# Linear attention into a gated feed-forward, one core: new loading of batch 0, one load queue in the order of need, and a reordered first output stage

## The chip, the cores and the metric

The kernel runs on one NeuronCore of one Trainium2 chip. A time is the duration of one execution on the device in microseconds (us). Five engines run side by side, each through its own list of instructions in order: PE (TensorE, matrix products), DVE (VectorE), ACT (ScalarE), POOL (GpSimd) and SP (SyncE, which here only issues transfers). Sixteen DMA engines move data between the chip's main memory and the on-chip memory. A transfer is issued by an engine and lands some us later; transfers that change the type on the way (fp32 in memory, bf16 on chip) are issued by POOL in this kernel, plain ones by SP.

Times in the texts below are positions on the trace of one profiled execution, counted from its first instruction.

## What is computed

Linear attention with the feature map phi(x) = elu(x) + 1 over 8 batches, 8 heads, 576 rows and head size 64, and then a feed-forward layer of width 2048 with a gate whose slope beta is a vector.

```python
def phi(x):
    return np.where(x > 0, x, np.exp(x) - 1.0) + 1.0
q_p, k_p = (phi(q), phi(k))
kv = np.einsum('bhsd,bhse->bhde', k_p, v)
z = np.sum(k_p, axis=2)
num = np.einsum('bhsd,bhde->bhse', q_p, kv)
den = np.einsum('bhsd,bhd->bhs', q_p, z)[..., None] + 1e-06
x = (num / den).transpose(0, 2, 1, 3).reshape(B * S, H * D)   # 4608 x 512
h = x @ w_in                                                   # 512 x 2048
g = h * (1.0 / (1.0 + np.exp(-beta * h)))
out = g @ w_out                                                # 2048 x 512
```

All inputs are fp32. The products run in bf16.

## The kernel before

Each batch has 576 rows: four tiles of 128 rows, and a fifth of 64 rows. The fifth tiles of the eight batches are gathered in `xT_tail` and run as a ninth batch. The stages of batch b are called here: phi (of k and q), kv (the product of phi(k) and v), numer (phi(q) times kv, divided), x_trans (x transposed), H (x times w_in, 16 tiles of `h_ps`, each put through Silu by ACT) and Y (g times w_out, four output tiles of 16 products each). From batch 2 on, the attention of the next batch is threaded into H of the current one, and its phi into Y. Batches 0 and 1 have an order written by hand.

The loads at the start, by SP and by POOL:

```python
k0f = stage[:, 0 : 4 * J * D]...               # fp32, in the buffer of w_out quarters 2 and 3
def load(eng, dst, src, b, h0=0, n=4): ...     # one transfer; h0, n: pairs of heads

for h0 in (0, 2):
    load(nc.sync, k0f, k, 0, h0, 2)
nc.sync.dma_start(out=beta_row, in_=moe_beta...)
nc.vector.memset(warm, 0.5)
...
make_identity(nc, identity)                    # on POOL
for h0 in (0, 2):
    load(nc.gpsimd, xq[0], q, 0, h0, 2)        # cast to bf16
for h0 in (0, 2):
    load(nc.gpsimd, vb[0], v, 0, h0, 2)
w_in_dma = [nc.gpsimd.dma_start(out=w_in_sb[i], ...) for i in range(4)]
load_w_out(0, w_in_dma[1])                     # SP, fp32, held until w_in quarter 1 is there
load_w_out(1)
hold(load(nc.gpsimd, xk[1], k, 1), w_in_dma[3])
q1_dma = load(nc.gpsimd, xq[1], q, 1)
load(nc.gpsimd, vb[1], v, 1)
```

The start of batch 0. `idle(n)` gives PE n products that nobody reads, to keep it from standing still:

```python
phi_step("k", 0, phi_part); phi_step("k", 1, phi_part)      # ACT: exp
idle(14)
phi_step("k", 0, phi_relu); phi_step("k", 0, phi_min)       # DVE
phi_step("q", 0, phi_part); ...                             # ACT
phi_step("k", 1, phi_relu)
w_out2_dma = load_w_out(2, q1_dma)                          # SP, held until q of batch 1 is there
load_w_out(3)
phi_step("k", 1, phi_min)
zt = [num0_tile() for _ in range(2)]
z_products(0, 0, zt)                                        # PE: sums of phi(k)
nc.tensor.matmul(bps, beta_row, ident16, is_transpose=True) # PE: beta to columns
idle(4)
z_products(0, 1, zt)
nc.vector.tensor_copy(beta_s, bps)                          # DVE, then three more small ones
...
phi_step("q", 0, phi_relu)
z_evac(zt)
phi_step("q", 0, phi_min)
phi_step("q", 1, phi_relu)
phi_step("q", 1, phi_min, 0, 4); phi_step("q", 1, phi_min, 4, J)
idle(10)
q_trans0(0); q_trans0(1)                                    # PE transposes, ACT copies
kv_direct(0, 0, kvp0)                                       # PE: phi(k) times v
for hh in range(2): kv_evac(0, hh, (0,), kvp0)              # DVE
q_trans0(2)
...                                                         # kv_direct, kv_evac of pair 1
dens(0, (0, 1), dps); recips(0, 2, P, dps)
q_trans0(3)
numer0(0, 0); numer0(0, 1)
...
x_trans(0, 0, nc.scalar)
...                                                         # then H of batch 0
```

Two PSUM pools matter later. `num0ps` has two banks and serves batches 0 and 1; `numps` takes their place from batch 2 on and holds one tile:

```python
def num0_tile():
    return num0ps.tile([P, 512], F32, tag="num0", name="nps0")   # bufs=2
def recips(t0, t1, n, dps):          # den and 1/den of row tiles t0 to t1, read from dps
    ...
def numer0(b, t):
    nps = num0_tile()
    ...                              # four products on PE
    norm(b, t, n, nps..., rden0[:n, t])   # DVE: nps times 1/den -> xs
def x_trans(b, t, eng): ...          # PE transposes xs; eng copies to xT
```

The stretch of Y of batch 0 and the attention of batch 1:

```python
w_out_scale(0, 0); w_out_scale(1, 0)          # DVE: w_out by 1/beta, to bf16
yps = [mm_tile("y_ps") for _ in range(4)]     # the four banks that h_ps uses too
phi_all(1, "k"); phi_all(1, "q")
for i in range(2):
    for t in range(4):
        y_mm(0, t, i, yps[t])                 # quarter i of the sum of output tile t
...                                           # z_products, z_evac of batch 1; loads of batch 2
for ts in ((0, 1), (2, 3)): q_trans(1, ts, num0_tile()..., (nc.scalar, nc.scalar))
for pr in range(2): kv_direct(1, pr, kv1)
w_out_scale(2, 0)
...                                           # kv_evac
dps1 = num0_tile()
q_trans(1, (4,), dps1..., (nc.scalar,))
y_mm(0, 0, 2, yps[0])
dens(1, range(NT), dps1)
recips(0, 4, P, dps1); recips(4, 5, G, dps1)
y_mm(0, 1, 2, yps[1])
numer0(1, 0); numer0(1, 1)
w_out_scale(3, 2)
...                                           # y_mm, x_trans, numer0 in turn
numer0(1, 4)
...
phi_part(2, "q", pr, ...); phi_relu; phi_min(2, "q", 0); phi_part(2, "k", 0, ...)
...
```

In H of batch 1, run after its tile 0: `q_trans_dma(2)` and `x_trans(1, 4, nc.vector)`; `numer(2, t)` runs after tiles 7, 9, 11, 13 and 15.

Of the kernel before, what the change touches and what calls it, by code (L numbers as in the profile page):

```python
# [16 lines left out]
def kernel(  # L17
# [55 lines left out]
        for a in vf  # L73
    ]

    k0f = stage[:, 0 : 4 * J * D].rearrange("p (h j d) -> p h j d", h=4, j=J)

    def load(eng, dst, src, b, h0=0, n=4):

        rows = src[b].rearrange("h (g j) d -> (h g) (j d)", j=J)  # L80
        return eng.dma_start(  # L81
            out=dst[:, h0 : h0 + n].rearrange("p h j d -> p h (j d)"),
            in_=rows.rearrange("(i p) e -> p i e", p=P)[:, h0 : h0 + n],
        )
# [3 lines left out]


    beta_row = consts.tile([FC, P], F32)  # L90
    for h0 in (0, 2):
        load(nc.sync, k0f, k, 0, h0, 2)
    nc.sync.dma_start(out=beta_row, in_=moe_beta.rearrange("(c p) -> c p", p=P))
    nc.vector.memset(warm, 0.5)  # L94
    tiny = consts.tile([P, 2], BF16)
# [2 lines left out]
    make_identity(nc, identity)  # L98
    ident16 = consts.tile([FC, FC], F32)
    make_identity(nc, ident16)  # L100
    for h0 in (0, 2):
        load(nc.gpsimd, xq[0], q, 0, h0, 2)
    for h0 in (0, 2):
        load(nc.gpsimd, vb[0], v, 0, h0, 2)

    w_in_v = moe_w_in.rearrange("(c p) f -> p c f", p=P)
    w_out_v = moe_w_out.rearrange("(c p) m -> p c m", p=P)
    w_in_dma = [
        nc.gpsimd.dma_start(out=w_in_sb[i], in_=w_in_v[:, :, i * 512 : (i + 1) * 512])  # L109
        for i in range(4)  # L110
    ]

    def load_w_out(i, after=None):
        d = nc.sync.dma_start(out=w_out_f[i], in_=w_out_v[:, i * 4 : (i + 1) * 4, :])
        if after is not None:
            hold(d, after)
        return d

    load_w_out(0, w_in_dma[1])
    load_w_out(1)  # L120
    hold(load(nc.gpsimd, xk[1], k, 1), w_in_dma[3])
    q1_dma = load(nc.gpsimd, xq[1], q, 1)
    load(nc.gpsimd, vb[1], v, 1)

    kvmask = consts.tile([P, 2, 2, EA], BF16)
    nc.vector.memset(kvmask, 0.0)
    nc.vector.memset(kvmask[:D, :, 0, :], 1.0)
    nc.vector.memset(kvmask[D:P, :, 1, :], 1.0)
    ones = consts.tile([P, 2], BF16)
    nc.vector.memset(ones, 1.0)  # L130
    for i in range(2):
        nc.vector.memset(vaug[i][:, :, :, :, D : D + 2], 1.0)

    warm_ps = mmps.tile([P, 512], F32, tag="mm", name="warm_ps")

# [29 lines left out]
        )  # L165

    def xin(b, a, pr):
        if b == 0 and a == "k":
            return k0f[:, 2 * pr : 2 * pr + 2]
        return (xk if a == "k" else xq)[b % NX][:, 2 * pr : 2 * pr + 2]  # L170

    def v_copy(eng, b, pr):
# [186 lines left out]
    def rows(b, j):  # L359
        return out[b * S : (b + 1) * S, :].rearrange("(g j) m -> j g m", j=J)[j]  # L360

    def y_out(b, t, yp, c0=0, c1=512, queues=(nc.sync, nc.sync)):
        y_sb = work.tile([P, DM], F32, tag="y_sb", name="y_sb", bufs=3)
        nc.vector.tensor_copy(y_sb[:, c0:c1], yp[:, c0:c1])  # L364
        for i in range(2):
            dst = rows(b, 2 * t + i) if b < B else rows(2 * t + i, J - 1)
            queues[i].dma_start(out=dst[:, c0:c1], in_=y_sb[i * G : (i + 1) * G, c0:c1])
# [74 lines left out]
    def phi_step(a, pr, f, *r):  # L442
        f(0, a, pr, *((xin(0, a, pr),) if f is not phi_min else ()), *r)
# [11 lines left out]
    phi_step("q", 1, phi_part, 0, 4)  # L455
    phi_step("q", 1, phi_part, 4, J)
    phi_step("k", 1, phi_relu)
    w_out2_dma = load_w_out(2, q1_dma)
    load_w_out(3)
    phi_step("k", 1, phi_min)  # L460
    zt = [num0_tile() for _ in range(2)]
    z_products(0, 0, zt)
# [9 lines left out]
    z_evac(zt)  # L472
    phi_step("q", 0, phi_min)
    phi_step("q", 1, phi_relu)
    phi_step("q", 1, phi_min, 0, 4)
    phi_step("q", 1, phi_min, 4, J)
    idle(10)
# [1 line left out]
    def q_trans0(t):  # L479
        q_trans(0, (t,), misc_bf()[:, 0 : 512 if t < NT - 1 else 256], (nc.scalar,))  # L480

    q_trans0(0)
    q_trans0(1)
    kv_direct(0, 0, kvp0)
    for hh in range(2):
        kv_evac(0, hh, (0,), kvp0)
    q_trans0(2)
    kvp1 = [num0_tile() for _ in range(2)]
    kv_direct(0, 1, kvp1)
    for hh in range(2):  # L490
        kv_evac(0, hh, (1,), kvp1)
    dens(0, (0, 1), dps)
    recips(0, 2, P, dps)
    q_trans0(3)
    numer0(0, 0)
    numer0(0, 1)
# [30 lines left out]
    def w_out_scale(i, n_act):  # L527
        for c in range(4):
# [3 lines left out]
            else:  # L532
# [2 lines left out]
                    None, ALU.mult,  # L535
                )

    nc.vector.reciprocal(rbeta, beta_c)
    w_out_scale(0, 0)
    w_out_scale(1, 0)  # L540
    yps = [mm_tile("y_ps") for _ in range(4)]
    phi_all(1, "k")
    phi_all(1, "q")
# [2 lines left out]
            y_mm(0, t, i, yps[t])  # L546
    kv1 = [miscps.tile([P, 512], F32, tag="misc", name="kv1") for _ in range(2)]
    kv_tile(1)
    for pr in range(2):
        z_products(1, pr, kv1)  # L550
    z_evac(kv1)
    hold(load(nc.gpsimd, xq[2], q, 2), w_out2_dma)
    load(nc.gpsimd, xk[2], k, 2)
    load(nc.gpsimd, vb[0], v, 2)

    for ts in ((0, 1), (2, 3)):
        q_trans(1, ts, num0_tile().bitcast(BF16), (nc.scalar, nc.scalar))
    for pr in range(2):
        kv_direct(1, pr, kv1)
    w_out_scale(2, 0)  # L560
    for hh in range(2):
        kv_evac(1, hh, (0, 1), kv1)
    dps1 = num0_tile()
    q_trans(1, (4,), dps1.bitcast(BF16)[:, 512:768], (nc.scalar,))
    y_mm(0, 0, 2, yps[0])
    dens(1, range(NT), dps1)
    recips(0, 4, P, dps1)
    recips(4, 5, G, dps1)
    y_mm(0, 1, 2, yps[1])
    numer0(1, 0)  # L570
    numer0(1, 1)
    w_out_scale(3, 2)
    y_mm(0, 2, 2, yps[2])
    x_trans(1, 0, nc.scalar)
    numer0(1, 2)
    y_mm(0, 3, 2, yps[3])
    x_trans(1, 1, nc.scalar)
    numer0(1, 3)
    y_mm(0, 0, 3, yps[0])
    y_out(0, 0, yps[0])  # L580
    x_trans(1, 2, nc.vector)
    numer0(1, 4)
    y_mm(0, 1, 3, yps[1])
    y_out(0, 1, yps[1])
    x_trans(1, 3, nc.vector)
    phi_tile(2, "q")
    phi_tile(2, "k")
    for pr in range(2):
        phi_part(2, "q", pr, xin(2, "q", pr))
    for pr in range(2):  # L590
        phi_relu(2, "q", pr, xin(2, "q", pr))
    phi_min(2, "q", 0)
    phi_part(2, "k", 0, xin(2, "k", 0))
    y_mm(0, 2, 3, yps[2])
    y_out(0, 2, yps[2])
    phi_min(2, "q", 1)
    phi_part(2, "k", 1, xin(2, "k", 1))
    y_mm(0, 3, 3, yps[3])
    y_out(0, 3, yps[3])
    for pr in range(2):  # L600
        phi_relu(2, "k", pr, xin(2, "k", pr))
    for pr in range(2):
# [36 lines left out]
    for b in range(1, B + 1):  # L639
        n = b + 1  # L640
        sh, sy = {}, {}
        if b == 1:
            at(sh, 0, lambda: q_trans_dma(2), lambda: x_trans(1, 4, nc.vector))
            at(sh, 1, lambda: [v_copy(nc.gpsimd, 2, pr) for pr in range(2)])
            at(sh, 2, lambda: load_kq(3, st[2, "qTd", "dma"]), lambda: load_v(3))
        if n < B:
            at(sh, 6 if b == 1 else 4, lambda: kv_both(n))
            for t in range(NT):
                at(sh, (7 if b == 1 else 5) + 2 * t, lambda t=t: numer(n, t))
                at(sh, min((8 if b == 1 else 6) + 2 * t, FC - 1), lambda t=t: x_trans_dma(n, t))  # L650
        if n + 1 < B:
            m = n + 1
            at(sy, 0, lambda: phi_all(m, "q"))
            at(sy, 2, lambda: q_trans_dma(m), lambda: load_kq(m + 1, st[m, "qTd", "dma"]))
            at(sy, 6, lambda: phi_all(m, "k"), lambda: [v_copy(nc.gpsimd, m, pr) for pr in range(2)])
            at(sy, 7, lambda: load_v(m + 1))
        h_phase(b, xT[b % 3] if b < B else xT_tail, sh)
        y_phase(b, sy, last=(b == B))
# [30 lines left out]
```

## Time and profile before

| | |
|---|---|
| time, median of 3 (range) | 295.34 us (294.95 to 295.96) |
| profiled execution, first to last instruction | 293.8 us |
| PE busy | 286.3 us, 97% |
| ACT, DVE, POOL busy | 159.7, 116.9, 33.4 us |
| read from main memory, written | 36.71 MB, 9.44 MB |
| H of batch 0 begins | 16.43 us |
| H of batch 1 begins | 52.84 us |
| Y of batch 1 begins | 70.82 us |
| one batch from there on | 30.06 us (Y at 70.82, 100.88, 130.94) |

A line of the timeline has the start, the duration, the engine, the line of the program, the operation, what it writes and reads, the size and the number of instructions merged into it; the bracket tells for how long the engine had stood idle and what ended that. A line of the waits names who waited for whom, the us in total, the number of waits and the longest. PE counts as busy while a product is in its pipeline, so "97% busy" does not say that PE had nothing to gain.

### The profile page before, as it was taken

The numbers are of one execution on the slowest core, as the hardware profiler recorded it, in microseconds if no ns is written. First come the engines' busy times: TensorE is split into PE (matmuls) and PEld (weight loads), VectorE is DVE, ScalarE is ACT, GpSimd is POOL, SyncE is SP. The second block draws the span as 40 slices with busy tenths as digits, with TensorE's granted clock in tenths as the row PEclk, the third lists the DMA queues.
The fourth block names the chain that finished last, engine by engine and source line by source line (L and its number), as shares of the span: only waits on it lengthen the run. The fifth ranks groups of instructions, "written<-read, shape, count | busy, mean of one in ns | idle before, by whom it ended". The sixth has DMA issues, their size and how long they took to land.

```text
span 293.8 us, 4725 instructions
## 1 busy us (share of the span) xinstructions
PE 286.3 (97%) x1881; PEld 142.7 (49%) x1881; DVE 116.9 (40%) x266; ACT 159.7 (54%) x208; POOL 33.4 (11%) x50
## 2 busy tenths in 40 slices
PE   7899999999999999999999999999999999999995
PEld 3584456445445444554455445544554444444443
DVE  5753478943734561356135522653251100110012
ACT  4658956855936772678167906690661077008500
POOL 9003020320050005000500053000000000000000
PEclk9999999999999999999999999999999999999999
DMA  7999989899389849942993199516131310131032
GB/s 200 201 214 331 201 282 197 194 250 183 74 211 252 137 52 269 238 73 59 247 247 66 49 232 255 94 34 164 38 71 44 74 37 0 36 74 36 0 71 73
DMA packets 51910, 40.82 MB, mean 139 GB/s; under 512 B 30752, under 2 KB 42288, under 8 KB 51888
## 3 DMA queue, kind: packets, MB, share of 16 engines
q1 hardware_dynamic: 40080, 27.68, 36.9%
q0 software_dynamic: 11648, 12.72, 26.3%
q8 instruction: 14, 0.23, 0.3%
q10 hardware_dynamic: 160, 0.13, 0.2%
q14 instruction: 8, 0.07, 0.1%
HBM read 36.71 MB, written 9.44 MB: 157 GB/s over the span
## 4 chain that ended last, share of the span: by engine, by line
PE 80%; DMA 13%; POOL 2%; DVE 2%; ACT 1%; issue 1%; SPq 0%; POOLq 0%
PE y_ps L352 39%; PE h_ps L334 35%; DMA w_in<-in_moe_w_in_dram 6%; DMA xq<-in_q_dram 3%; PE nps L285 2%; DMA stage<-in_moe_w_out_dram 2%; PE kvp L184 2%; DMA qTd<-phi_q 1%; ACT g L342 1%; POOL w_in L109 1%; POOL xq L81 1%; DVE w_out L533 1%; POOL vf L81 0%; PE nps L432 0%; ACT L342 0%
## 5 line engine op out<-in xcount | busy, mean ns | idle before, releaser
L342 ACT ACTIVATE g<-h_ps,beta_c 128x512 bf16<-128x512 f32 x144 | 97.9, 688 | 100.4 <-PE h_ps L334 100.4
L352 PE MATMUL y_ps<-w_out,g 128*128 128x512 bf16 (+2 forms) x592 | 127.5, 373 | 0.6 <-DVE w_out L533 0.5
L334 PE MATMUL h_ps<-xT,w_in 128*128 128x512 bf16 (+1 forms) x560 | 118.6, 361 | 0.3 <-DVE y_sb L364 0.2
L352 PEld LDWEIGHTS <-g 128*128 128x128 bf16 x592 | 57.3, 98 | 66.2 <-issue 1.2
L334 PEld LDWEIGHTS <-w_in 128*128 128x128 bf16 x624 | 56.5, 98 | 58.6 <-issue 0.7
L364 DVE COPY y_sb<-y_ps 128x512 f32<-128x512 f32 (+2 forms) x37 | 24.9, 674 | 84.1 <-PE y_ps L352 83.5
L299 DVE TENSOR_TENSOR xs<-nps,rden 128x512 bf16<-128x512 f32 (+1 forms) x40 | 27.2, 686 | 5.1 <-DMA xT<-xs 2.7
L81 POOL DMA_DIRECT2D xk<-in_k_dram x7 | 5.4, 769 | 119.0 <-DMA qTd<-phi_q 77.6
L149 ACT ACTIVATE e<-xq 128x1152 bf16<-128x1152 bf16 (+2 forms) x17 | 17.9, 1098 | 1.3 <-DMA xq<-in_q_dram 1.2
L160 DVE TENSOR_TENSOR phi_q<-e,r 128x1152 bf16<-128x1152 bf16 (+2 forms) x17 | 12.2, 722 | 15.3 <-ACT e L149 15.1
L149 ACT ACTIVATE e<-xk 128x1152 bf16<-128x1152 bf16 x14 | 15.5, 1150 | 1.3 <-DVE phi_q L160 1.1
L234 DVE TENSOR_TENSOR kv_bd<-kvp,kvmask 128x260 bf16<-128x260 f32 x12 | 4.6, 424 | 25.7 <-PE kvp L184 25.7
L293 DVE TENSOR_SCALAR den<-nps 128x8 f32<-128x8 f32 (+1 forms) x30 | 4.9, 165 | 23.5 <-PE nps L285 23.5
L334 PE MATMUL h_ps<-xT_tail,w_in 128*128 128x512 bf16 x64 | 14.0, 379 | 0.0
L285 PEld LDWEIGHTS <-qTd 128*128 128x128 bf16 x120 | 9.4, 98 | 8.0 <-DMA qTd<-phi_q 0.9
L160 DVE TENSOR_TENSOR phi_k<-e,r 128x1152 bf16<-128x1152 bf16 x16 | 11.5, 752 | 3.6 <-ACT e L149 3.5
L285 PE MATMUL nps<-kv_bd,qTd 128*128 128x130 bf16 x120 | 12.1, 221 | 0.7 <-DMA qTd<-phi_q 0.7
L174 POOL CAST vaug<-vf 128x1152 bf16<-128x1152 f32 x10 | 11.2, 1158 | 3.9 <-DMA vf<-in_v_dram 3.9
L138 PE MATMUL warm_ps<-warm 128*128 128x512 bf16 x28 | 8.3, 456 | 1.5 <-DVE warm L94 1.5
L149 ACT ACT_TABLE_LOAD x6 | 7.7, 1283 | 2.9 <-DMA xq<-in_q_dram 2.8
L342 ACT ACT_TABLE_LOAD x7 | 9.0, 1283 | 0.1
L81 POOL DMA_DIRECT2D xq<-in_q_dram x9 | 6.8, 754 | 14.9 <-DMA stage<-in_moe_w_out_dram 14.9
(67 smaller groups left out, 104.2 us busy)
## 6 DMA issues: line engine op xcount, KB each, us to landing
out_dram<-y_sb SPq DMA_DIRECT2D x70, 128.0 KB, 2.5
vf<-in_v_dram SPq DMA_DIRECT2D x5, 1152.0 KB, 7.3
xk<-in_k_dram POOLq DMA_DIRECT2D x7, 576.0 KB, 10.2
xq<-in_q_dram POOLq DMA_DIRECT2D x7, 576.0 KB, 12.4
w_in<-in_moe_w_in_dram POOLq DMA_DIRECT2D x4, 512.0 KB, 13.4
g<-in_moe_w_out_dram SPq DMA_DIRECT2D x2, 1024.0 KB, 9.5
stage<-in_moe_w_out_dram SPq DMA_DIRECT2D x2, 1024.0 KB, 8.4
stage<-in_k_dram SPq DMA_DIRECT2D x2, 576.0 KB, 4.4
```

What stands on the lines that cost most here:

```text
L81: return eng.dma_start(out=dst[:, h0 : h0 + n].rearrange("p h j d -> p h (j d)"), in_=rows.rearrange("(i p) e -> p i e", p=P)[:, h0 : h0 + n],
L138: nc.tensor.matmul(warm_ps[:, 0:cols], warm[:, 0:P], warm[:, 0:cols], start=True, stop=True)
L149: nc.scalar.activation(st[b, a, pr, "e"][:, :, j0:j1], x[:, :, j0:j1], ACTF.Exp)
L160: nc.vector.tensor_tensor(st[b, a][:, pr, j0:j1].rearrange("p j (h d) -> p j h d", h=2), st[b, a, pr, "e"][:, :, j0:j1].rearrange("p h j d ...
L174: eng.tensor_copy(vaug[b % 2][:, pr, :, :, 0:D], src[:, 2 * pr : 2 * pr + 2].rearrange("p h j d -> p j h d"),)
L184: nc.tensor.matmul(ps[hh, pr], st[b, "k"][r, pr, j, :], vaug[b % 2][r, pr, j, :, 0:EA], start=(j == 0), stop=(j == J - 1), skip_group_chec ...
L285: nc.tensor.matmul(nps[: qs.shape[-1], hh, pr * 2 * EA : (pr + 1) * 2 * EA], qs, st[b, "kv"][:, hh, pr, :], start=True, stop=True, skip_gr ...
L299: nc.vector.tensor_mul(xs[:n].rearrange("p i a d -> p a i d"), num, rd[:, :, :, None].to_broadcast([n, 2, 4, D]),)
L334: nc.tensor.matmul(hp[:, c0:c1], w_in_sb[ff // 4][:, kc, (ff % 4) * P : (ff % 4 + 1) * P], x[:, kc, c0:c1], start=(kc == 0), stop=(kc == K ...
L342: nc.scalar.activation(g_sb[b % 2][:, ff, :], hp, ACTF.Silu, scale=beta_c[:, ff : ff + 1])
L352: nc.tensor.matmul(yp[:, c0:c1], g_sb[b % 2][:, ff, t * P : (t + 1) * P], w_out_sb[i][:, c, c0:c1], start=(ff == 0), stop=(ff == FC - 1), ...
L364: nc.vector.tensor_copy(y_sb[:, c0:c1], yp[:, c0:c1])
```

## The change

Batch 0's k and q are both loaded as fp32 by SP, one behind the other, and beta behind them. Everything else is loaded by POOL in the order in which it is needed: v of batch 0, w_in, the first three quarters of w_out, k and q of batch 1, the last quarter of w_out, v of batch 1, then batch 2. The holds between transfers are gone. The mask `kvmask` is filled by POOL instead of DVE. In batch 0 the denominators of the first two row tiles move ahead of the second half of kv. In Y of batch 0, the third quarter of the sums comes before and around the attention of batch 1 and the fourth is spread through it; ACT takes over the output copy of tile 1; the denominator and numerator of the fifth row tile of batch 1 move to the end of the stretch, behind phi(q) of batch 2. `numer` of batch 2 moves two tiles later in H of batch 1. The purpose is to have data at hand when it is needed and PE free of waits in the first 70 us.

```diff
+    q0f = g_f[:, 0 : 4 * J * D].rearrange("p (h j d) -> p h j d", h=4, j=J)
...
-    for h0 in (0, 2):
-        load(nc.sync, k0f, k, 0, h0, 2)
+    for dst, src in ((k0f, k), (q0f, q)):
+        for h0 in (0, 2):
+            load(nc.sync, dst, src, 0, h0, 2)
     nc.sync.dma_start(out=beta_row, in_=moe_beta.rearrange("(c p) -> c p", p=P))
...
-    for h0 in (0, 2):
-        load(nc.gpsimd, xq[0], q, 0, h0, 2)
...
-    load_w_out(0, w_in_dma[1])
-    load_w_out(1)
-    hold(load(nc.gpsimd, xk[1], k, 1), w_in_dma[3])
-    q1_dma = load(nc.gpsimd, xq[1], q, 1)
-    load(nc.gpsimd, vb[1], v, 1)
-    nc.vector.memset(kvmask, 0.0)                # and two more
+    nc.gpsimd.memset(kvmask, 0.0)                # and two more, ahead of the loads of v
...
     phi_step("k", 1, phi_relu)
-    w_out2_dma = load_w_out(2, q1_dma)
-    load_w_out(3)
     phi_step("k", 1, phi_min)
...
     phi_step("q", 1, phi_relu)
+    for i in range(3):
+        load_w_out(i)                            # now by POOL
+    load(nc.gpsimd, xk[1], k, 1)
+    load(nc.gpsimd, xq[1], q, 1)
+    load_w_out(3)
+    load(nc.gpsimd, vb[1], v, 1)
...
-    q_trans0(0)
-    q_trans0(1)
+    for t in range(3):
+        q_trans0(t)
     kv_direct(0, 0, kvp0)
...
-    q_trans0(2)
+    dens(0, (0, 1), dps)
+    recips(0, 2, P, dps)
...                                              # kv_direct and kv_evac of pair 1
-    dens(0, (0, 1), dps)
-    recips(0, 2, P, dps)
...
+    load(nc.gpsimd, xq[2], q, 2)
+    load(nc.gpsimd, xk[2], k, 2)
+    load(nc.gpsimd, vb[0], v, 2)
     nc.vector.reciprocal(rbeta, beta_c)
-    w_out_scale(0, 0)
-    w_out_scale(1, 0)
+    for i in range(3):
+        w_out_scale(i, 0)
...
+    y_mm(0, 0, 2, yps[0])
+    y_mm(0, 1, 2, yps[1])
     for pr in range(2):
         z_products(1, pr, kv1)
     z_evac(kv1)
-    hold(load(nc.gpsimd, xq[2], q, 2), w_out2_dma)
...
+    w_out_scale(3, 0)
+    y_mm(0, 2, 2, yps[2])
+    y_mm(0, 3, 2, yps[3])
     for ts in ((0, 1), (2, 3)):
         q_trans(1, ts, num0_tile().bitcast(BF16), (nc.scalar, nc.scalar))
+    y_mm(0, 0, 3, yps[0])
+    y_out(0, 0, yps[0])
     for pr in range(2):
         kv_direct(1, pr, kv1)
-    w_out_scale(2, 0)
+    dps1 = num0_tile()
+    q_trans(1, (4,), dps1.bitcast(BF16)[:, 512:768], (nc.scalar,))
     for hh in range(2):
         kv_evac(1, hh, (0, 1), kv1)
...
     dens(1, range(NT), dps1)
     recips(0, 4, P, dps1)
-    recips(4, 5, G, dps1)
-    y_mm(0, 1, 2, yps[1])
+    y_mm(0, 1, 3, yps[1])
+    y_out(0, 1, yps[1], copier=nc.scalar)
     numer0(1, 0)
     numer0(1, 1)
-    w_out_scale(3, 2)
...
+    phi_part(2, "q", 0, xin(2, "q", 0))
+    y_mm(0, 2, 3, yps[2], 0, 256)
     x_trans(1, 0, nc.scalar)
     numer0(1, 2)
+    phi_part(2, "q", 1, xin(2, "q", 1))
+    y_mm(0, 2, 3, yps[2], 256, 512)
+    x_trans(1, 1, nc.vector)
     numer0(1, 3)
+    y_mm(0, 3, 3, yps[3], 0, 256)
     x_trans(1, 2, nc.vector)
+    y_mm(0, 3, 3, yps[3], 256, 512)
+    x_trans(1, 3, nc.vector)
+    y_out(0, 2, yps[2])
+    y_out(0, 3, yps[3])
+    for pr in range(2):
+        phi_part(2, "k", pr, xin(2, "k", pr))
+        phi_relu(2, "q", pr, xin(2, "q", pr))
+        phi_min(2, "q", pr)
+    recips(4, 5, G, dps1)
+    numer0(1, 4)
...
-    at(sh, (7 if b == 1 else 5) + 2 * t, lambda t=t: numer(n, t))
-    at(sh, min((8 if b == 1 else 6) + 2 * t, FC - 1), lambda t=t: x_trans_dma(n, t))
+    at(sh, min((9 if b == 1 else 5) + 2 * t, FC - 1), lambda t=t: numer(n, t))
+    at(sh, min((10 if b == 1 else 6) + 2 * t, FC - 1), lambda t=t: x_trans_dma(n, t))
```

## The prediction

> **What bounds the kernel now.** I read the page first, then the chain of waits in order of time, then PE's own waits, then the timelines of PE, DVE and ACT for the first 72 us. From 70.82 us on, the chain is PE alone, 30.06 us for a batch, with no wait: nothing that the change touches lies there. All that can be won or lost is in the first 70.8 us, and PE is busy there nearly throughout:
>
> ```profile
> PE 286.3 (97%) x1881; PEld 142.7 (49%) x1881; DVE 116.9 (40%) x266; ACT 159.7 (54%) x208; POOL 33.4 (11%) x50
> ```
>
> The view of PE's waits before 72 us lists all that PE itself stands for:
>
> ```profile
> PE nps L285 <- DMA qTd<-phi_q: 0.7, 1, 0.7
> PE nps L195 <- DVE phi_k L160: 0.6, 1, 0.6
> PE y_ps L352 <- DVE w_out L533: 0.5, 2, 0.3
> PE tp L253 <- DVE phi_q L160: 0.2, 1, 0.2
> PE h_ps L334 <- DVE y_sb L364: 0.2, 1, 0.2
> ```
>
> Together 2.2 us. That is nearly all a better order of loads can give back, besides an earlier start of H of batch 0. The start is set by a chain through k, q and beta; its lines in the timeline:
>
> ```profile
> 6.51 1.16 ACT L149 ACTIVATE e<-stage 128x1152 bf16<-128x1152 f32 x1 [0.96 <-DMA stage<-in_k_dram]
> 6.79 0.20 PE L464 MATMUL bps<-ident,beta_row 16*128 16x16 f32 x1
> 8.38 0.17 DVE L467 COPY beta_s<-bps 128x16 f32<-128x16 f32 x1
> 9.09 0.45 DVE L153 TENSOR_SCALAR r<-xq 128x1152 bf16<-128x1152 bf16 x1
> 10.44 0.45 DVE L153 TENSOR_SCALAR r<-xq 128x1152 bf16<-128x1152 bf16 x1
> 11.48 0.51 PE L253 MATMUL tp<-identity,phi_q 128*128 128x128 bf16 x6 [0.21 <-DVE phi_q L160]
> 13.93 0.65 PE L432 MATMUL nps<-kv_bd,qT 128*128 128x128 bf16 x8
> 16.43 1.05 PE L334 MATMUL h_ps<-xT,w_in 128*128 128x128 bf16 x16
> ```
>
> The reader is to see the order: on PE the transposition of beta stands before the second group of z products, and on DVE the four small beta operations (8.38 to 9.09) stand before every phi operation on q. Today beta is there at 6.65 us (issued at 1.75, 4.9 us to landing), and nobody waits for it. The seam of batches 0 and 1 matters too:
>
> ```profile
> 45.38 0.63 PE L432 MATMUL nps<-kv_bd,qT 128*128 128x128 bf16 x8
> 50.49 0.67 DVE L299 TENSOR_TENSOR xs<-nps,rden 64x512 bf16<-64x512 f32 x1
> 53.55 1.16 ACT L149 ACTIVATE e<-xk 128x1152 bf16<-128x1152 bf16 x1 [1.11 <-DVE phi_q L160]
> 53.80 0.29 PE L315 MATMUL xtp<-identity,xs 64*128 64x64 bf16 x4
> ```
>
> Numerators of two tiles run back to back (x8), and the fifth tile's xs is ready (50.49) 3 us before PE transposes it inside H of batch 1 (53.80).
>
> [...]
>
> **The change part by part.**
>
> Loads of batch 0. k's halves are there at 4.38 and 6.51 us. q's halves follow on the same ring; at 1.5 us (590 KB at 400 GB/s) to 2.1 us a half they land by 8.0 to 8.6 and 9.5 to 10.8, against 8.57 and 10.08 now: nothing gained. Beta landed 0.15 us behind k's second half; I put it at about 10.0. Then step by step: transposition of beta 10.0 to 10.2; four DVE operations 0.8, to 11.0; relu of q 0.75 (fp32), to 11.75. On PE, idle(4) and the z products end at 10.2 + 0.9 + 0.4 = 11.5, so the z evacuation takes 11.75 to 12.05; min 0.7, to 12.7; relu 0.8, to 13.5; first part of min 0.4, to 13.9. PE's transposes behind it start at 14.0 instead of 11.48: +2.5. PE meanwhile stands from 6.8 to 10.0 for beta, a wait that is not there today.
>
> Order in batch 0. q_trans0(2) now precedes kv_direct, and needs the bank that ACT's first copy frees: copy 14.35 to 14.9, transposes 15.0 to 15.3, kv_direct 15.3 to 15.9, where today it starts 0.45 us behind the transposes. Evacuation 16.0 to 16.45, den and 1/den 16.45 to 16.9, evacuation of the second pair to 17.4, numerators 17.4 instead of 13.93 (+3.5); with 1/den already there norm starts 0.3 sooner. H of batch 0 starts at about 19.6 instead of 16.43: +3.2.
>
> Loads of everything else. One queue at 400 GB/s, with no holds, delivers the source bytes back to back: v 1.2, w_in 4.2, w_out 1.05 each, k, q, v 1.2 each. From 8.4 us: w_out quarter 2 at about 31, k 34, q 37, w_out quarter 3 39, v 42, batch 2 at 45, 48, 51. Needed (H of batch 0 ends at 19.6 + 15.5 = 35.2) at 44, 38, 40, 44, 48, 53, 56, 58. Every load is early: the two waits for w_out go, -0.5.
>
> Y of batch 0. By PE's pieces from the trace (16 products 3.45, z 0.55, 16 transposes 1.0, kv_direct 1.08, dens 0.59, a numerator 0.23): 35.2, eight groups to 42.1, two to 43.8, z 44.4, two 46.1, transposes 47.1, one group 48.0, kv_direct 49.05. dens follow the transposes of tile 4 with nothing between, and wait for ACT's copy until 49.85; one group to 51.3. Then a point that only the bank numbers show: recips(4, 5) moved behind the last norms, so dps1 keeps one of the two num0 banks, and all five numerators of batch 1 share the other. Each waits for the norm of the one before, 1.1 us a round (0.23, 0.69, two handovers): 51.3, 52.4, 53.5, 54.6. The third and fourth x copies end at 56.5. H of batch 1 starts at 56.6. From H of batch 0 to H of batch 1 that is 37.0 us, against 52.84 - 16.43 = 36.4: +0.6 with the -0.5 inside.
>
> H of batch 1. Its tile 0 takes 0.9 us, to 57.5; then PE must transpose the fifth tile, whose norm stands on DVE behind two y copies (1.3), two relu and two min of q (2.3) and den, 1/den, norm (1.0): from 56.5 to 61.1. PE stands 3.6 us. ACT's exp of k needs a buffer that the first min frees, then a table load of 1.28: Silu starts at 61.4, hidden behind that wait. kv and `numer` of batch 2 no longer wait for the transposed q: -0.7, and -0.2 for y_sb. But tiles 3 and 4 of `numer` both fall on tile 15 (the min in the diff), and numps holds one tile: PE waits for den, 1/den and norm, +1.2. A hand sum of this phase: today 17.98; after 0.9 + 3.6 + 0.2 + 15 x 0.864 + 1.16 + 5 x 0.23 + 1.2 = 21.2: +3.2.
>
> Sum: 3.2 + 0.6 + 3.2 = +7.0 us. 295.3 + 7.0 = 302.3; I say 302.0.
>
> **The rivals.** First, beta could land early: it is 8 KB, and if the engines take rings by turns or its packets slip in between, it is there at 7 to 8 us. Then DVE's chain starts with q's landing, H of batch 0 slips by only 0.5 to 1.5 us, and the time is 299 to 300. For it speaks how soon beta now follows k; against it that it followed k and did not overtake it. Second, the author's purpose: the loads bind, and the single queue in the order of need frees PE. For it speak the DMA shares near full until 43 us and the w_out wait; against it that PE's waits for data sum to 1.2 us, and that every wait named above is for an order of instructions, not for data. If the new orders cost nothing, 293 to 294. Third, POOL's v transfers may share the engines with q's halves from about 5 us on; then q and beta land 2 us later and the time is near 304. [...]
>
> **Range and chances.** The seam terms (3.2 and 0.6) follow from orders and banks, which I trust to about 1 us together; the start (3.2) hangs on beta, with -2 and +2. So 299.0 to 305.0. 2% lies at 301.25, a little below my middle: slower 0.62, same 0.36, faster 0.02.
>
> **What would show it.** PE waiting for beta's landing from about 6.8 to 10 us; H of batch 0 first seen near 19.6; numerators of batch 1 as five groups of four, about 1.1 us apart; a PE wait of 3 us or more for xs right after tile 0 of H of batch 1; a wait of about 1.2 us before Y of batch 1; from there 30.06 us a batch as before. I am wrong if beta is early, if the fifth tile's norm runs before phi of q, or if H of batch 0 starts at or before 16.4.

## The result, and the profile after

| | before | after |
|---|---|---|
| time, median | 295.14 us (294.61 to 295.96) | 311.14 us (310.97 to 311.45) |
| ratio | 1 | 1.0541, 95% interval 1.0514 to 1.0568 |
| start to H of batch 0 | 16.43 us | 24.13 us (+7.7) |
| H of batch 0 to H of batch 1 | 36.41 us | 37.46 us (+1.05) |
| H of batch 1 to Y of batch 1 | 17.82 us | 24.36 us (+6.5) |
| from there to the end | 223.14 us | 223.24 us |
| trace, sum | 293.8 us | 309.2 us |

The change made the kernel 5.4% slower. I had predicted 302.0 us and a range of 299.0 to 305.0. The four stretches run from the first product of one stage to the first of the next, so they add up to the span of the trace; the loss lies in the first three, and the steady part, two thirds of the time, is as it was. (The first product of Y of batch 1 in the kernel before begins at 70.66 us; the 70.82 given above is where the chain of waits has it.)

The page's line of busy time for the kernel after, and its row of TensorE's granted clock, the share of its full clock that it was given, in 40 equal slices of the span, in tenths:

```profile
PE 291.4 (94%) x1889; PEld 145.0 (47%) x1889; DVE 116.5 (38%) x265; ACT 158.9 (51%) x206; POOL 35.5 (11%) x55
...
PEclk9689999968999999999999999999999999999999
```

PE is busy for 5.1 us *more* than before, with the same work; eight products are now cut into two halves each, hence x1889 for x1881. The second line says why: twice the clock falls (6, 8, and again 6, 8), so that the same products take longer and count as more busy time. PE's waits in the first 90 us of the kernel after:

```profile
PE bps L451 <- DMA beta_row<-in_moe_beta_dram: 5.2, 1, 5.2
PE xtp L304 <- DVE xs L288: 3.7, 1, 3.7
...
PE nps L274 <- DVE xs L288: 1.2, 1, 1.2
PE nps L421 <- DVE xs L288: 0.8, 1, 0.8
PE nps L403 <- ACT qT L229: 0.5, 1, 0.5
PE tp L242 <- ACT qT L229: 0.5, 1, 0.5
```

Each of these six is a wait that was not there before: beta's landing, the fifth tile's norm, the double numerator of batch 2, the shared num0 bank, ACT's copy ahead of dens, and in batch 0 the bank that ACT's first copy frees for q_trans0(2). The waits of before (w_out, the transposed q, y_sb) are gone; they were 1.4 us. The start of the kernel after, from the timelines of ACT, PE and DVE:

```profile
9.52 1.16 ACT L138 ACTIVATE e<-g 128x1152 bf16<-128x1152 f32 x1 [2.48 <-DMA g<-in_q_dram]
12.58 1.26 ACT L138 ACTIVATE e<-g 128x512 bf16<-128x512 f32 x2 [1.90 <-DMA g<-in_q_dram]
12.84 0.26 PE L451 MATMUL bps<-ident,beta_row 16*128 16x16 f32 x1 [5.21 <-DMA beta_row<-in_moe_beta_dram]
13.13 0.17 DVE L454 COPY beta_s<-bps 128x16 f32<-128x16 f32 x1 [5.25 <-PE bps L451]
13.85 0.75 DVE L142 TENSOR_SCALAR r<-g 128x1152 bf16<-128x1152 f32 x1
16.16 0.75 DVE L142 TENSOR_SCALAR r<-g 128x1152 bf16<-128x1152 f32 x1
18.30 0.61 PE L242 MATMUL tp<-identity,phi_q 128*128 128x128 bf16 x8
21.62 0.65 PE L421 MATMUL nps<-kv_bd,qT 128*128 128x128 bf16 x8
24.13 1.05 PE L323 MATMUL h_ps<-xT,w_in 128*128 128x128 bf16 x16
```

q's halves land at 9.5 and 12.5 us instead of 8.6 and 10.0, beta at 12.7 instead of 6.7; the rest of the chain hangs on beta, whose transposition begins at 12.84, as the bracket of beta_s shows: DVE stood 5.25 us for it, with q's first half already there. And the seam of batches 0 and 1 after, from PE and DVE:

```profile
55.83 0.40 PE L421 MATMUL nps<-kv_bd,qT 128*128 128x128 bf16 x4
57.01 0.40 PE L421 MATMUL nps<-kv_bd,qT 128*128 128x128 bf16 x4 [0.78 <-DVE xs L288]
...
65.60 0.68 DVE L288 TENSOR_TENSOR xs<-nps,rden 64x512 bf16<-64x512 f32 x1
...
66.34 0.39 PE L304 MATMUL xtp<-identity,xs 64*128 64x64 bf16 x4 [3.72 <-DVE xs L288]
66.66 7.85 PE L323 MATMUL h_ps<-xT,w_in 128*128 128x512 bf16 x24
```

The numerators come one at a time (x4, 1.2 us apart) where they came as x8; the fifth tile's xs is ready only at 66.3; and the 24 products behind the wait take 7.85 us: the first 12 follow each other at about 427 ns, the rest at 216 ns.

### The profile page after: what moved, and what is told of

The parts are those of the page before. It is cut to its first block, busy times and chain, and to the rows that moved or that the text cites. A ratio compares the mean times of both kernels' runs of the same rounds, so it can differ in the third digit from the quotient of the medians.

```text
span 309.2 us, 4741 instructions
## 1 busy us (share of the span) xinstructions
PE 291.4 (94%) x1889; PEld 145.0 (47%) x1889; DVE 116.5 (38%) x265; ACT 158.9 (51%) x206; POOL 35.5 (11%) x55
## 4 chain that ended last, share of the span: by engine, by line
PE 91%; DMA 3%; DVE 3%; ACT 1%; SPq 1%; issue 1%; DVEq 0%
PE h_ps L323 41%; PE y_ps L341 40%; DMA beta_row<-in_moe_beta_dram 3%; PE nps L274 2%; PE kvp L173 2%; PE warm_ps L127 2%; DVE xs L288 1%; PE nps L421 1%; PE xtp L304 1%; SPq L83 1%; PE kv L184 1%; DVE y_sb L231 1%; DVE phi_q L149 0%; ACT qT L229 0%; PE nps L242 0%
## 5 line engine op out<-in xcount | busy, mean ns | idle before, releaser
L341 PE MATMUL y_ps<-w_out,g 128*128 128x512 bf16 (+3 forms) x600 | 127.0, 371 | 0.0
L323 PE MATMUL h_ps<-xT,w_in 128*128 128x512 bf16 (+1 forms) x560 | 120.8, 366 | 0.3 <-DVE xT L311 0.2
L341 PEld LDWEIGHTS <-g 128*128 128x128 bf16 x600 | 58.1, 98 | 65.2
L231 DVE COPY y_sb<-y_ps 128x512 f32<-128x512 f32 (+2 forms) x36 | 24.2, 674 | 89.3 <-PE y_ps L341 89.3
L138 ACT ACTIVATE e<-xq 128x1152 bf16<-128x1152 bf16 x14 | 15.6, 1156 | 0.1
L149 DVE TENSOR_TENSOR phi_k<-e,r 128x1152 bf16<-128x1152 bf16 x16 | 11.5, 751 | 6.6 <-ACT e L138 6.5
L127 PE MATMUL warm_ps<-warm 128*128 128x512 bf16 x28 | 11.0, 570 | 1.5 <-DVE warm L97 1.5
L163 POOL CAST vaug<-vf 128x1152 bf16<-128x1152 f32 x10 | 11.2, 1159 | 1.9 <-DMA vf<-in_v_dram 1.9
L173 PEld LDWEIGHTS <-phi_k 64*128 64x128 bf16 x216 | 6.3, 94 | 2.5 <-issue 2.5
## 6 DMA issues: line engine op xcount, KB each, us to landing
xk<-in_k_dram POOLq DMA_DIRECT2D x7, 576.0 KB, 10.2
```

The costliest lines, as they stand in the source:

```text
L127: nc.tensor.matmul(warm_ps[:, 0:cols], warm[:, 0:P], warm[:, 0:cols], start=True, stop=True)
L138: nc.scalar.activation(st[b, a, pr, "e"][:, :, j0:j1], x[:, :, j0:j1], ACTF.Exp)
L149: nc.vector.tensor_tensor(st[b, a][:, pr, j0:j1].rearrange("p j (h d) -> p j h d", h=2), st[b, a, pr, "e"][:, :, j0:j1].rearrange("p h j d ...
L163: eng.tensor_copy(vaug[b % 2][:, pr, :, :, 0:D], src[:, 2 * pr : 2 * pr + 2].rearrange("p h j d -> p j h d"),)
L173: nc.tensor.matmul(ps[hh, pr], st[b, "k"][r, pr, j, :], vaug[b % 2][r, pr, j, :, 0:EA], start=(j == 0), stop=(j == J - 1), skip_group_chec ...
L231: eng.tensor_copy(dst, src)
```

## The experiments

Fifteen kernels were run, each with a median of at least four executions. Within one edit the times scatter by 0.5 to 3.7 us, so I compare stretches of the traces where a mechanism is at stake, and use times for verdicts; a trace shows one of the executions, and not always one near the median. All numbers in us; the ratio is to the kernel before, measured beside each run. H0 and H1 are the first products of H of batch 0 and 1, Y1 that of Y of batch 1:

| run | time | ratio (95% interval) | to H0 | H0 to H1 | H1 to Y1 |
|---|---|---|---|---|---|
| before | 295.14 | 1 | 16.43 | 36.41 | 17.82 |
| after | 311.14 | 1.0541 (1.0514 to 1.0568) | 24.13 | 37.46 | 24.36 |
| fill_beta | 308.62 | 1.0463 (1.0420 to 1.0505) | 21.39 | 37.46 | 23.12 |
| fill_t5 | 308.29 | 1.0456 (1.0433 to 1.0478) | 23.84 | 37.46 | 21.76 |
| beta_first | 308.63 | 1.0474 (1.0442 to 1.0505) | 21.28 | 38.15 | 23.13 |
| v_behind | 307.97 | 1.0435 (1.0389 to 1.0481) | 19.24 | 37.46 | 24.13 |
| bank | 308.06 | 1.0426 (1.0379 to 1.0473) | 23.87 | 36.24 | 22.95 |
| norm4 | 305.76 | 1.0343 (1.0294 to 1.0392) | 24.36 | 36.23 | 20.42 |
| numback | 309.31 | 1.0461 (1.0404 to 1.0518) | 24.87 | 37.45 | 23.18 |
| combo | 304.82 | 1.0312 (1.0261 to 1.0363) | 21.33 | 38.30 | 20.71 |
| front_back | 303.51 | 1.0275 (1.0234 to 1.0317) | 16.55 | 37.57 | 24.10 |
| norm4_e4 | 303.87 | 1.0279 (1.0237 to 1.0322) | 23.46 | 36.24 | 18.03 |
| best | 295.92 | 1.0016 (0.9999 to 1.0033) | 16.64 | 36.35 | 17.54 |
| queue_only | 297.33 | 1.0072 (1.0050 to 1.0093) | 16.28 | 39.12 | 17.11 |
| order0 | 296.62 | 1.0043 (1.0029 to 1.0056) | 17.78 | 36.24 | 17.44 |
| q_sync | 296.19 | 1.0029 (1.0009 to 1.0048) | 16.89 | 36.35 | 17.54 |
| best2 | 295.57 | 1.0008 (0.9994 to 1.0022) | 16.45 | 36.34 | 17.24 |

**fill_beta.** Does the stand for beta cost only its own length?

```diff
+    idle(23)
     nc.tensor.matmul(bps, beta_row, ident16, is_transpose=True, ...)
```

> The changed kernel with 23 idle products (5.0 us) put on TensorE ahead of the transposition of beta, so that it works instead of standing while beta is on its way; beta itself comes as late as before (12.8 us). Theory A (the stand of 5.2 us costs twice: the wait, and 6.8 us of halved clock after it, which stretches the idle products and the z products that VectorE waits for): the clock stays at 1.0 to the transposes, these start at 16.9 instead of 18.3 us, H of batch 0 at 22.7 instead of 24.1, time 309.7. Rival B (only the landing of beta counts): unchanged, 311.1.

PE's timeline in this run:

```profile
6.73 5.14 PE L127 MATMUL warm_ps<-warm 128*128 128x512 bf16 x22
11.80 0.23 PE L452 MATMUL bps<-ident,beta_row 16*128 16x16 f32 x1
21.39 1.05 PE L323 MATMUL h_ps<-xT,w_in 128*128 128x128 bf16 x16
```

The clock stayed at 1.0 through the start, and H of batch 0 came at 21.39. In this trace beta landed 1.5 us sooner (11.2), and its transposition, behind the idle products, began 1.0 us sooner (11.80), so the cleaner measure is from there to H of batch 0: 9.59 us against 11.29. Theory A: 1.7 us of the start are the halved clock. The size varies: the stretch took 10.8 to 12.3 us in the six traces whose start is that of the kernel after (after, fill_t5, bank, norm4, norm4_e4, numback), all with a halved clock in it, and 9.6 to 9.7 in the two of fill_beta and v_behind, which have none. With the clock full, the chain from beta on takes the 9.6 us that the prediction had worked out for it.

**fill_t5.** The same question for the fifth tile.

```diff
-    at(sh, 0, lambda: q_trans_dma(2), lambda: x_trans(1, 4, nc.vector))
+    at(sh, 0, lambda: q_trans_dma(2), fill, lambda: x_trans(1, 4, nc.vector))   # fill: 17 idle products
```

> The changed kernel with 17 idle products (3.7 us) between tile 0 of H of batch 1 and the transposition of the fifth row tile, so that TensorE works during that wait. Theory A (a halved clock follows the stand and stretches 12 to 24 products of H): the transposition stays at 66.3 us, the 24 products behind it take 216 ns each instead of 327, time 308.5. Rival B (H is slow there because Silu comes late and h_ps has four banks): unchanged, 311.1.

PE's timeline in this run:

```profile
62.16 3.83 PE L632 MATMUL fill_ps<-warm 128*128 128x512 bf16 x17
66.04 0.29 PE L304 MATMUL xtp<-identity,xs 64*128 64x64 bf16 x4
66.26 5.35 PE L323 MATMUL h_ps<-xT,w_in 128*128 128x512 bf16 x24
```

The transposition is no earlier (4.7 us after H of batch 1 began, as in after), yet the 24 products behind it take 5.35 us instead of 7.85. Theory A holds: 2.6 us of this stretch were the clock (24.36 to 21.76), and doing useless work won them, 308.29 against 311.14.

**beta_first.**

```diff
-    for dst, src in ((k0f, k), (q0f, q)): ...
+    for h0 in (0, 2): load(nc.sync, k0f, k, 0, h0, 2)
     nc.sync.dma_start(out=beta_row, ...)
+    for h0 in (0, 2): load(nc.sync, q0f, q, 0, h0, 2)
```

> The changed kernel with the load of beta issued between k and q instead of behind q. Theory A (beta's place in SyncE's ring is what moved the start): beta is transposed at 7.7 us, the chain on VectorE then waits for q's second half (12.5 us, unchanged), transposes at 13.8, H of batch 0 at 19.6 instead of 24.1, time 306.6. Rival B (v of batch 0, which shares the engines with q, is the cause; beta is only along for the ride): q's landing alone holds the chain and the gain is under 1 us, 310.5.

The first steps came as theory A had them (bps at 6.95, the transposes behind min at 13.90), but H of batch 0 at 21.28 instead of 19.6, and 308.63 instead of 306.6. The missing part is again the clock:

```profile
11.52 0.29 PE L243 MATMUL tp<-identity,phi_q 128*128 128x128 bf16 x2 [0.78 <-DVE phi_q L150]
13.90 0.51 PE L243 MATMUL tp<-identity,phi_q 128*128 128x128 bf16 x6 [2.10 <-DVE phi_q L150]
```

PE waited 0.8 and then 2.1 us for phi of q, and from 15.9 us on it ran at half speed for 6.8 us. A wait taken out at one place came back as a wait for q, because q's second half still landed at 12.5.

**v_behind.**

```diff
-    for h0 in (0, 2): load(nc.gpsimd, vb[0], v, 0, h0, 2)
+    for h0 in (0, 2):
+        d = load(nc.gpsimd, vb[0], v, 0, h0, 2)
+        if h0 == 0: hold(d, q0_dma[0])              # q's first half has landed
```

> The changed kernel with v of batch 0 held until the first half of q has landed; beta still behind q. Theory A (rings are taken by turns: v takes half of the engines from 6 us on and so delays q's second half and beta by 3 us): q at 7.6 and 9.3, beta at 9.6, H of batch 0 at 19.3, time 306.3. Rival B (q is slow for another reason, such as fp32 rows into that buffer): q and beta land as late as before, and v later, 311 to 313.

From the timelines of ACT and PE in this run:

```profile
7.75 1.16 ACT L140 ACTIVATE e<-g 128x1152 bf16<-128x1152 f32 x1 [0.67 <-DMA g<-in_q_dram]
9.37 1.26 ACT L140 ACTIVATE e<-g 128x512 bf16<-128x512 f32 x2 [0.46 <-DMA g<-in_q_dram]
9.57 0.21 PE L453 MATMUL bps<-ident,beta_row 16*128 16x16 f32 x1 [2.75 <-DMA beta_row<-in_moe_beta_dram]
```

With v out of the way q's second half and beta land 3.2 us sooner, and H of batch 0 begins at 19.24: theory A on all three counts (9.3, 9.6, 19.3 expected). The median, 307.97, is 1.7 us above the 306.3 expected; the trace is of the fastest execution, 305.81. This is the start that I had predicted (beta 10.0, H at 19.6). So the predicted chain was right and beta's landing was not: v, issued by GpSimd meanwhile, takes its share of the engines. The traces show it: 3.0 us lie between the landings of q's halves where v runs beside and 1.6 where not, and from 7 to 10 us of the kernel after, the 16 engines began 82 to 88 packets of SyncE's queue and 77 to 91 of GpSimd's in each us. How an engine chooses its next packet is not shown; that the rings are taken by turns was my assumption in the expectation.

**bank, norm4, numback.** The seam, part by part: bank moves only recips(4, 5); norm4 moves the fifth norm as well; numback puts the numerators of batch 2 where they were.

```diff
 # bank                                    # norm4: bank, and
     recips(0, 4, P, dps1)                       x_trans(1, 3, nc.vector)
+    recips(4, 5, G, dps1)                 +     numer0(1, 4)
...                                              y_out(0, 2, yps[2])
-    recips(4, 5, G, dps1)                 ...
     numer0(1, 4)                          -     numer0(1, 4)
 # numback
-    at(sh, min((9 if b == 1 else 5) + 2 * t, FC - 1), lambda t=t: numer(n, t))
+    at(sh, (7 if b == 1 else 5) + 2 * t, lambda t=t: numer(n, t))     # x_trans_dma likewise at 8
```

> The changed kernel with recips(4, 5) put back right behind recips(0, 4); the fifth tile's numerator and norm stay at the end. Theory A (dps1 keeps one of two banks, so the numerators of batch 1 go one by one, and the fifth norm behind phi of q is a separate, larger cost): the first two numerators run back to back again, H of batch 1 begins 0.8 us sooner, the 3.7 us wait for the fifth tile stays, time 310.3. Rival B (the bank is the cause of the whole seam): the wait for the fifth tile shrinks too, 306.

> The changed kernel with recips(4, 5) right behind recips(0, 4) and the fifth tile's numerator and norm right behind its fourth transposition, ahead of the output copies and of phi of q of batch 2 on VectorE. Theory A: the wait of 3.7 us in H of batch 1 goes, with it the halved clock behind it (2.6 us) and the bank's 0.8 us: 304.0. Rival B (the wait moves to the next link, the buffers of exp and Silu's late start): 307 to 308.

> The changed kernel with the numerators of batch 2 behind tiles 7, 9, 11, 13 and 15 of H of batch 1 as before. Theory A (two of them behind tile 15 cost one round of norm, 1.2 us): 309.9. Rival B (the later place was needed for the transposed q): a new wait at tile 7, no gain, 311.

bank: the numerators run as x8 again, and H0 to H1 shrinks by 1.2 us, not 0.8, to 36.24; the wait for the fifth tile stays, at 3.2 us. So theory A in kind. H1 to Y1 fell by 1.4 us too, more than the 0.5 us of shorter wait: the halved clock lasted 3.4 us in this run and not 6.8, and so the time is 308.06 and not the 310.3 of the expectation. norm4: 305.76 lies between the two theories. The wait for the fifth tile is gone, but a new one stands in its place. From PE's waits and ACT's timeline of norm4:

```profile
PE h_ps L323 <- ACT g L331: 2.3, 1, 2.3
```

```profile
59.33 1.16 ACT L138 ACTIVATE e<-xk 128x1152 bf16<-128x1152 bf16 x1
63.61 1.16 ACT L138 ACTIVATE e<-xk 128x1152 bf16<-128x1152 bf16 x1 [3.12 <-DVE phi_q L149]
64.79 1.28 ACT L331 ACT_TABLE_LOAD   x1
```

ACT waits 3.12 us between two exp of k, for a min of q on DVE, whose input buffer it needs; Silu starts late, h_ps's four banks fill up, and PE waits. In the kernel after this was hidden behind the larger wait. numback: H1 to Y1 is 1.2 us shorter, and no wait at tile 7 appears: theory A.

**combo.** beta_first, v_behind, norm4 and numback at once.

> The changed kernel with four mends at once: beta between k and q, v of batch 0 held until q's first half has landed, the fifth tile's norm and recips(4, 5) early as in the run norm4, numerators of batch 2 as before. If the loss is these four orders and nothing else, H of batch 0 starts at 16.5 us, H of batch 1 at 53, Y of batch 1 at 70.2, time 294 to 295, level with the kernel before. If the single load queue or the new order of Y has a cost of its own, 297 or more.

304.82, 10 us above the expectation: a miss that taught most. PE waits 2.3 us for Silu as in norm4, and a new one stands in the start:

```profile
PE h_ps L325 <- ACT g L333: 2.3, 1, 2.3
PE nps L186 <- DMA vf<-in_v_dram: 2.1, 1, 2.1
```

With beta and q early, v, held behind q, is now last, and its 2.1 us bring the halved clock once more: 10.2 us long, from 15.4 on, over the first tiles of H. My holding of v was too late by that much.

**front_back.** The other way round: only the start is undone.

```diff
-    for dst, src in ((k0f, k), (q0f, q)): ...                  # q by SyncE, fp32
+    for h0 in (0, 2): load(nc.sync, k0f, k, 0, h0, 2)
+    for h0 in (0, 2): load(nc.gpsimd, xq[0], q, 0, h0, 2)      # ahead of v
...                                                             # kvmask by VectorE, order of batch 0 as before
```

> The changed kernel with only its start undone: q of batch 0 again by GpSimd as bf16 ahead of v, beta right behind k, kvmask by VectorE, the order of batch 0 as in the kernel before. Everything from H of batch 0 on is the changed kernel's. Theory A (the start alone cost 7.7 us): H of batch 0 at 16.5 us, the rest as in the changed kernel (37.5 to H of batch 1, 23 to 24.4 to Y of batch 1), time 302 to 303.5. Rival B (the single queue, one load longer again, now brings w_in or w_out late): a wait for data in H or Y of batch 0, 305 or more.

H of batch 0 at 16.55, the two other stretches as in after (37.57, 24.10), 303.51: the start alone is 7.6 us. The losses add up, since each stands in a stretch of its own.

**norm4_e4.**

```diff
-    ... tag="e", name="e", bufs=3)        -    ... tag="r", name="r", bufs=3)
+    ... tag="e", name="e", bufs=4)        +    ... tag="r", name="r", bufs=2)
```

> The run norm4 with four buffers instead of three for the result of exp (and two instead of three for relu, to make room). Theory A (the 2.3 us for which TensorE waited for Silu there come from exp of k waiting 3.1 us for a buffer that the first min of q frees): exp of k runs at once, Silu starts at 61.8 instead of 66.1 us, the wait goes, from H of batch 1 to Y of batch 1 18.0 instead of 20.4 us, time 303.3. Rival B (Silu is late for its banks or its table): no change, 305.8.

ACT's timeline in this run:

```profile
58.43 2.21 ACT L138 ACTIVATE e<-xk 128x1152 bf16<-128x1152 bf16 x2
60.66 1.28 ACT L331 ACT_TABLE_LOAD   x1
61.96 2.42 ACT L331 ACTIVATE g<-h_ps,beta_c 128x512 bf16<-128x512 f32 x4
```

Both exp run on end, Silu starts at 61.96, and H1 to Y1 is 18.03: theory A to 0.1 us. 303.87 as time.

**best.** front_back, norm4, numback and four exp buffers together: what stays of the change is the single load queue and the new order of Y.

> The changed kernel with its start undone, the fifth tile's norm early, the numerators of batch 2 as before, and four buffers for exp: what is left of the change is the single load queue and the new order of Y of batch 0. Parts: H of batch 0 at 16.4, 36.2 to H of batch 1, 16.7 to Y of batch 1, 223.2 from there: 292.5 on the trace, 294.2 as time, 0.8 us under the kernel before. If the queue or the order costs something that the other losses hid, 296 or more.

295.92, ratio 1.0016 with an interval that touches 1: level with before, 1.7 us above the sum. One of the parts was off: H1 to Y1 took 17.54 instead of 16.7, because PE waits at tile 7 after all once the seam is short:

```profile
PE nps L275 <- DMA qTd<-phi_q: 0.7, 1, 0.7
```

Another 0.5 us lies at the very end: the last output lands 2.5 us behind the last product in best and in q_sync alike, but from the last product to the end of the trace it is 4.2 us in best and 3.7 in q_sync, with nothing changed there. What takes it is not shown.

**queue_only.** The kernel before with the new load queue and nothing else.

```diff
-    load_w_out(0, w_in_dma[1]); load_w_out(1)                   # SyncE
-    hold(load(nc.gpsimd, xk[1], k, 1), w_in_dma[3]) ...
+    for i in range(3): load_w_out(i)                            # GpSimd
+    load(nc.gpsimd, xk[1], k, 1); load(nc.gpsimd, xq[1], q, 1)
+    load_w_out(3); load(nc.gpsimd, vb[1], v, 1)                 # then batch 2, without the hold
```

> The kernel before with nothing changed but the loads from w_in on: all of w_out by GpSimd in the order of need, its third quarter ahead of batch 1, no holds. Theory A (the order of the loads is worth the two waits for w_out, 0.5 us): 36.4 becomes 35.9 from H of batch 0 to H of batch 1, time 294.6. Rival B (fp32 loads through GpSimd's queue are slower or delay k and q of batch 1): a wait before the z products of batch 1, 296 or more.

Slower by 0.7%. PE's waits in its first 72 us:

```profile
PE nps L242 <- DVE phi_q L149: 1.3, 2, 0.9
PE kv L184 <- DVE w_out L526: 0.7, 1, 0.7
```

Rival B in effect: with a third quarter of w_out ahead of them, k and q of batch 1 land at 34.5 and 37.3 us instead of 31.7 and 34.6, and phi of q is not ready when the old order transposes it, and the clock halves behind it (from 42.9 us, 3.4 us). The queue needs the new order of Y, which puts the third quarter's products there. The two together are neutral (best), apart the queue costs; the new order of Y with the old queue was not run.

**order0, q_sync, best2.** Three variants of best: with the change's order of batch 0; with q as fp32 by SyncE, beta ahead of it and v held for k only; with the numerators of batch 2 one tile later.

```diff
 # order0                         # q_sync                                        # best2
-    q_trans0(0); q_trans0(1)     +    load(nc.sync, q0f, q, 0, h0, 2)            -    (7 if b == 1 else 5) + 2 * t
+    for t in range(3):           +    if h0 == 0: hold(d, k0_dma[1])             +    min((8 if b == 1 else 5) + 2 * t, FC - 1)
+        q_trans0(t)              -    load(nc.gpsimd, xq[0], q, 0, h0, 2)
     kv_direct(0, 0, kvp0)
...
+    dens(0, (0, 1), dps); recips(0, 2, P, dps)      # ahead of kv_direct(0, 1)
```

> The run best with one more part of the change put back in: the order of batch 0 (three transpositions of q ahead of kv, the first denominators between its halves). Theory A (my hand schedule: kv waits for the bank that the first copy frees, which costs more than the early denominator brings): H of batch 0 at 17.1 instead of 16.6 us, time 296.4. Rival B (the order is neutral or helps): 16.3 to 16.6, 295.9 or less.

> The run best with q of batch 0 as fp32 by SyncE again, but beta issued between k and q, v held until k's second half has landed, kvmask by GpSimd, order of batch 0 as in best. It asks what the new way of loading q is worth when neither beta nor v is in its way. Theory A (nothing: q lands at 7.7 and 9.4 us instead of 8.6 and 10.0, but its fp32 relu takes 0.3 us longer each, and v lands later): H of batch 0 between 16.2 and 16.9 us, time 295.5 to 296.3. Rival B (v becomes the new wait, and its stand brings the halved clock): 17.5 or later, 297 or more.

> The run best with the numerators of batch 2 behind tiles 8, 10, 12, 14 and 15 of H of batch 1 instead of 7, 9, 11, 13 and 15. In best TensorE waits 0.7 us for the transposed q at tile 7. Theory A: that wait goes, a wait of 0.3 us between the last two numerators comes, from H to Y of batch 1 17.2 instead of 17.5, time 295.5. Rival B (the last two cost the whole round of 1.2 us): 18.0, 296.4.

order0: H of batch 0 at 17.78, 1.1 us later: theory A, with twice the size. q_sync: H at 16.89, ratio 1.0029 (1.0009 to 1.0048): loading q by SyncE brings nothing even with its way free. best2: the wait for the transposed q is gone, 0.4 us for the last norm came, 17.24 as expected; 295.57, ratio 1.0008 (0.9994 to 1.0022), level with before. No version measured beat the kernel before.

## Why the prediction was wrong

The direction and every wait named were right; the sum, +7.0, was less than half of the +15.4 on the trace. By its own steps; beta's landing failed, and the sum has no term for the clock:

**Loads of batch 0: the step that failed.** "I put it at about 10.0": beta landed at 12.7, behind q's second half (12.5), and was transposed at 12.84 (11.5 to 13.2 in the six traces with this start). The prediction let q run at full rate on its ring and left v's share of the engines to the third rival ("q and beta land 2 us later"); it was 3.2 us (v_behind), and it was the main case: v's transfers are issued at 2.3 us and its packets flow from 6.6 us on, in the middle of q. The sum's 0.75 us for relu of q from fp32 stands in no trace of before (k took 0.81 and 1.06 us there, and q from bf16 0.45); the kernel after has 0.75 at 13.85 and at 16.16.

**The clock: not in the sum, and the larger loss.** The two stands of PE that I had foreseen (3.2 and 3.6 us) are in the sum with their own length alone. In the kernel after, the clock is halved for 6.8 us at each of them (10.31 to 17.14 and 64.92 to 71.75 us), and that cost 1.7 us (fill_beta) and 2.6 us (fill_t5): behind the fifth tile 12 products follow each other at 427 ns instead of 216. With the clock the start has 3.2 + 2.8 for beta + 1.7, against +7.7, and the third stretch 3.2 + 2.6, against +6.5; the last 0.7 us was not taken apart.

**Order in batch 0.** Right in kind; 1.1 us by order0, where the prediction has about 0.7 (from +2.5 at the transposes to +3.2 at H).

**Loads of everything else.** Right: no wait for data after the start, and the w_out waits are gone. The 400 GB/s of its estimates is what fp32 moves at when it flows alone: 401 GB/s from 24 to 27 us of the kernel before (SyncE), 392 from 24 to 28 of the kernel after (GpSimd). That the loads would be early and still bring nothing was also right (best), and queue_only shows the order of Y to be their condition.

**Y of batch 0.** The shared bank and ACT's copy (0.5 us for 0.8) came in kind, +1.05 for +0.6 predicted; the bank alone is 1.2 us (bank), so without it the new order would be 0.2 us ahead of the old one.

**H of batch 1.** The wait for the fifth tile (3.7 for 3.6) and the double numerator (1.2 for 1.2) came within 0.1 us. "Silu starts at 61.4, hidden behind that wait" was right too (4.9 us behind the first product of H of batch 1, for 4.8), and norm4 shows what it hid: 2.3 us.

**The rivals.** Beta slipping in early did not happen. The author's purpose, loads that bind, is refuted: best has the new queue and the new order of Y without the losses, and is level. The third came in full, 3.2 us for 2.

## What to carry to other kernels

A transfer that many small steps wait for, like these 8 KB of beta, is issued ahead of the large ones of its engine (ahead of q, beta was transposed at 6.95 us instead of 12.84); count what other issuers send to the same engines when you place its landing (v cost q's second half and beta 3.2 us). A foreseen stand of TensorE of some us is to be priced twice, once as itself and once as the slow clock that may follow it (here 5.2 and 3.7 us, and 1.7 and 2.6 us more); useless products in the gap won the second part (308.62 and 308.29 us for 311.14). When an operation is moved later, look for the tile it keeps alive and for the next engine in order behind it: here one late `recips` held a PSUM bank and one late norm stopped TensorE, and each mend uncovered the wait behind it.

## What was not expected of the hardware

The clock was halved behind short waits too: in the start of beta_first no wait was longer than 2.1 us, and from 15.89 us on the clock was halved for 6.8 us; in queue_only PE's longest wait after its first product was 0.9 us, and the clock was halved from 42.87 to 46.28 us. In fourteen traces (all but order0, q_sync and best2), taken over their first 86 us in stretches of 3.41 us on a grid of each trace's own, every stretch has one granted clock throughout, 1.00 or 0.50. Lines of the view by stretches, one for each of four stretches, from after, v_behind, combo and beta_first (columns: from and to, length, busy time of PE, PEld, DVE, ACT, POOL, granted clock, DMA share, GB/s):

```profile
61.51:64.92 3.41, 1.02 (x4) 0.29 (x3) 3.20 (x7) 0.93 (x1) 0.00 (x0) 1.00 0.43 100
```

```profile
4.94:8.35 3.41, 1.79 (x25) 0.74 (x23) 2.44 (x4) 2.42 (x3) 0.33 (x1) 1.00 0.99 372
```

```profile
11.99:15.40 3.41, 1.62 (x36) 1.29 (x35) 1.00 (x5) 1.64 (x3) 3.41 (x6) 1.00 1.08 131
```

```profile
12.48:15.89 3.41, 1.54 (x32) 1.21 (x33) 1.68 (x4) 2.90 (x5) 1.72 (x3) 1.00 1.24 207
```

PE was busy for 1.02, 1.79, 1.62 and 1.54 of the 3.41 us. After the first, third and fourth the clock was halved; after the second it stayed. Over the fourteen traces, the 17 stretches at full clock with PE busy for up to 1.62 us were each followed by half clock, and none with 1.79 us or more was. This is a count, and does not settle what is counted: in the last us of norm4_e4 a stretch with PE busy for 1.45 us was followed by full clock. What ends the half clock is open as well: a stretch at half clock with PE busy for 2.89 us was followed by full clock (fill_beta, 63.08 us), one of 3.14 by another half (combo, 18.82 us).

The grid does not begin at the same time in each trace: the first stretch read begins at 4.28 us in bank, 5.08 in before, 6.90 in after and 7.34 in norm4. A wait of much the same length was followed by more or less of half clock: behind the fifth tile it was 6.8 us in after (wait of 3.7 us) and 3.4 in bank (3.2 us); that this hangs on where the wait falls in the grid is my reading. The times of one edit scatter with the clock: the four executions of v_behind took 305.81, 307.80, 308.13 and 308.94 us at a mean granted clock of 0.989, 0.983, 0.983 and 0.978.
